# Taking the decision on the range checks ahead of the last products, with an order of pieces from a table

## The chip, the cores and the metric

The kernel runs on one core of a Trainium2 chip. Its engines work side by side and are released by semaphores: TensorE (matmuls), VectorE, ScalarE and GpSimd (elementwise work), SyncE (which issues the transfers). The metric is the time of one execution on the device in microseconds; the median of three runs before the change was 409.76 us (409.35 to 410.42). One further execution was profiled, and its span is 408.4 us.

## The reference

Attention over four batches, eight heads, 768 positions and 64 elements per head, with a causal window of 128 positions and four sink positions that every query sees, and behind it a gated unit that mixes along the positions. All tensors are float32.

```
scores = q @ k.T / sqrt(64)           # kept: sinks (pos < 4), and 0 <= rel < 128
x      = softmax(scores) @ v          # heads side by side: (4, 768, 512)
h      = max(x @ w_in, 0)             # w_in 512 x 1024
u, v   = h[..., :512], h[..., 512:]
v_n    = (v - mean(v)) / sqrt(var(v) + 1e-6)
v_s    = w_spatial @ v_n + b_spatial[:, None]   # along the 768 positions
out    = (u * v_s) @ w_out            # w_out 512 x 512
```

## The kernel before

The kernel has two paths. The fast path assumes four sinks, a window of 128 and values in a range in which a pair of half-precision numbers, a high part and a rest, can stand for a float32: a product is then three half-precision matmuls (high by high, high by rest, rest by high; `three`, line 744). The pairs are made by elementwise operations: the high part is a cast (line 713 on ScalarE, 722 on GpSimd, one of VectorE's own), the rest is a subtraction (line 729, on VectorE or GpSimd). The general path (`general_path`, line 71) does everything in float32 and is taken only if a check fails.

The fast path works through the batches and through tiles of 128 positions: scores against the window and the sinks (`sc`, line 1027 and 1033), a masked maximum in one VectorE pass (`pexp`, `nm`, line 1038), the exponential on ScalarE, the split of the weights (`p`), their transposition, the product with the values (`av`), division (`x`), and the two halves of the hidden layer (`ps_v`, `ps_u`). When a batch is complete, the product along the positions (`ps_s`, on 128x256 tiles), the gate (`g`, lines 1275 and 1279), the product with w_out (`ps_o`, 12 matmuls for one tile of 128 positions), ScalarE's copy of it (`ob`, line 1301) and the store (line 1302) follow. `ps_v`, `ps_u`, `ps_s`, `ps_o` and the small results of the checks share two banks of PSUM in turn; `ob` has three buffers.

The range checks (`checks`, line 874) gather maxima and sums. Their end is a chain: `all_max` (line 772) finds the largest gate bound with a matmul into `ps_row` (line 780), a reduction on VectorE (784), a matmul into `ps_col` (787) and a copy (791); `late` compares (897 to 900); `count` adds the marks of all partitions with a matmul (903); `decide` (908 to 914) turns them into one integer, `flagi`. After the fast path every engine reads `flagi` into a register (line 1370) and `tc.If` (line 1371) branches over the general path.

What sets the order: every operation is a piece in the class `Plan`, with a rank, the engines it can run on, a duration on each by a model, the tiles it reads and writes, and the function that emits it. `forward` (line 391) lists the pieces in the order in which a model of the engines, of the buffers, of a shared port and of TensorE's clock would take them, the lowest priority number first, and picks the engine for pieces that can run on several. `settle` (line 541) calls it with widening tolerance. In `order` (line 520) the priorities are the ranks at first; then a list of 120 seeds, `PASSES`, scatters them and `backward` (line 489) replaces them by distances to the end, 161 times in all. The functions are then called in the resulting order under a manual schedule. 24 pieces of four `idle` matmuls each (line 1310) may be put in where the plan has nothing for TensorE.

Of the kernel before, what the change touches and what calls it, by code (L numbers as in the profile page):

```python
# [270 lines left out]
CHECKS_AT = 56.0  # L271
COLD_TIMES, DMA_START, DMA_LAND = 2.0, 1.7, 1.5
# [4 lines left out]
PASSES = ((360001144, 275, 149, 2), (360001145, 532, 116, 3), (360001147, 406, 76, 2), (360001148, 636, 53, 4), (360001094, 148, 0, 2), (360001096, 596, 486, 4), (360001098, 13, 170, 1), (360001101, 565, 463, 3), (360001223, 680, 71, 3), (360001233, 210, 0, 2), (360001254, 0, 242, 4), (360001255, 0, 145, 5), (360001275, 0, 627, 4), (360001389, 1103, 11, 4), (360001407, 165, 0, 2), (360001474, 33, 0, 5), (360001509, 242, 108, 3), (360001612, 0, 216, 2), (360001663, 0, 118, 1), (360001619, 305, 0, 4), (370001122, 81, 0, 0), (370001124, 68, 0, 0), (370001138, 0, 23, 2), (370001140, 0, 51, 0), (370001149, 60, 0, 0), (370001150, 80, 0, 0), (370001153, 159, 4, 0), (370001154, 207, 37, 0), (370001160, 0, 48, 0), (370001161, 0, 90, 0), (370001162, 0, 115, 0), (370001163, 0, 116, 0), (370001168, 63, 0, 0), (370001171, 157, 0, 0), (370001174, 82, 0, 0), (370001175, 356, 0, 0), (370001178, 121, 79, 0), (370001181, 33, 31, 0), (370001197, 83, 0, 0), (370001198, 22, 0, 0), (370001201, 246, 141, 0), (370001204, 36, 82, 0), (370001206, 138, 136, 0), (370001216, 90, 0, 0), (370001279, 20, 20, 0), (370001296, 256, 89, 0), (370001312, 136, 0, 0), (370001330, 0, 86, 0), (370001374, 3, 4, 0), (370001379, 0, 45, 0), (370001419, 90, 24, 0), (370001423, 115, 98, 0), (370001426, 0, 44, 0), (370001955, 0, 54, 0), (370001960, 284, 0, 0), (370001962, 316, 0, 0), (370001964, 38, 0, 0), (370002082, 101, 0, 0), (370002095, 127, 277, 0), (370002206, 59, 0, 0), (372001153, 0, 24, 0), (372001159, 0, 90, 0), (372001181, 0, 69, 0), (372001191, 184, 0, 0), (372001263, 14, 0, 0), (372001285, 171, 0, 0), (372001297, 0, 90, 0), (372001303, 0, 14, 0), (372001313, 103, 36, 0), (372001322, 0, 74, 0), (372001324, 0, 46, 0), (372001326, 0, 129, 0), (372001327, 0, 125, 0), (372001334, 55, 0, 0), (372001436, 114, 25, 0), (372001441, 0, 28, 0), (372001451, 311, 0, 0), (372001463, 91, 136, 0), (372001543, 0, 9, 0), (372001544, 44, 0, 0), (372001561, 0, 67, 0), (372001566, 0, 184, 0), (372001572, 131, 0, 0), (372001576, 33, 198, 0), (372001583, 138, 45, 0), (372001663, 0, 13, 0), (372001696, 382, 212, 0), (372001701, 337, 19, 0), (372001708, 0, 24, 0), (372001727, 281, 120, 0), (372001797, 277, 74, 0), (372001807, 0, 109, 0), (372001808, 120, 0, 0), (372001817, 193, 94, 0), (372001820, 105, 86, 0), (372001824, 0, 88, 0), (372001826, 0, 104, 0), (372001837, 274, 0, 0), (372001847, 78, 81, 0), (372001929, 72, 0, 0), (379001144, 260, 0, 0), (379001145, 180, 0, 0), (379001239, 0, 33, 0), (379001867, 105, 0, 0), (379001876, 197, 27, 0), (379001902, 192, 11, 0), (379001904, 0, 38, 0), (379002017, 87, 57, 0), (379002028, 0, 173, 0), (379002029, 0, 30, 0), (379002031, 0, 53, 0), (379002044, 214, 29, 0), (379002126, 0, 19, 0), (379002155, 47, 0, 0), (379002158, 250, 0, 0), (379002163, 191, 80, 0), (379002302, 51, 0, 0), (379002303, 177, 0, 0), (379002414, 0, 109, 0), (379002429, 48, 187, 0),)  # L277
NAMES = ("PE", "d", "a", "p", "SP")
# [30 lines left out]


def scatter(seed, i):

    if seed >> 5 & 1 and mix(seed + 555, i) < 0.4:
        return 0.0
    return mix(seed, i)


def near(seed, x):

    if seed >> 6 & 1:  # L320
        return 1.0
    u = (mix(seed, 7) + 1) / 2
    return 1.0 if abs(x - u * u * 430.0) < 5.0 + 20.0 * (mix(seed, 8) + 1) else 0.0


def mix(seed, i):
    x = (seed * 2654435761 + i * 40503 + 12345) & 0xFFFFFFFF
    x ^= x >> 16
    x = x * 2246822519 & 0xFFFFFFFF
    x ^= x >> 13  # L330
    x = x * 3266489917 & 0xFFFFFFFF
    x ^= x >> 16
    return (x & 0xFFFF) / 65536.0 + (x >> 16) / 65536.0 - 1.0


class Plan:
# [54 lines left out]
    def forward(self, prio, ahead, most):  # L391
        ps, n = self.ps, len(self.ps)
        missing, ready = list(self.missing), [0.0] * n
        left = {b: len(u) for b, u in self.users.items()}
        until, taken, since, after = dict.fromkeys(self.users, 0.0), set(), {}, {}
# [6 lines left out]
        follow = [list(x) for x in self.after]  # L402
# [18 lines left out]
        while open_:  # L421
# [38 lines left out]
            for base, ring in self.tiles[i]:  # L460
                if base in taken:
                    if base in after:
                        for j in self.users[after[base]]:
                            follow[j].append(i)
                else:
# [4 lines left out]
                    if slots[ring][k]:  # L470
                        after[base] = slots[ring][k]
                        for j in self.users[slots[ring][k]]:
                            follow[j].append(i)
                    slots[ring][k] = base
# [11 lines left out]
        self.last = start, length, lag, engine, order, follow  # L486
        return max(until.values())

    def backward(self):
        start, length, lag, engine, order, follow = self.last  # L490
        n = len(order)
        earlier, missing = [[] for _ in range(n)], [0] * n
        for i, x in enumerate(follow):
            x = set(x)
            x.discard(i)
            missing[i] = len(x)
            for j in sorted(x):
                earlier[j].append(i)
        ready, free, to_end = [0.0] * n, dict.fromkeys(NAMES, 0.0), [0.0] * n
        open_ = [i for i in range(n) if not missing[i]]  # L500
        for i in open_:
            ready[i] = lag[i]
        while open_:
            best = None
            for i in open_:
                t = max(ready[i], free[engine[i]])
                if best is None or t < best[0] - 1e-9 or (t < best[0] + 1e-9 and start[i] + length[i] > start[best[1]] + length[best[1]]):
                    best = (t, i)
            t, i = best
            to_end[i] = free[engine[i]] = t + length[i]  # L510
            open_.remove(i)
            for j in earlier[i]:
                ready[j] = max(ready[j], to_end[i] + lag[j])
                missing[j] -= 1
                if not missing[j]:
                    open_.append(j)
        last = max(to_end)
        return [last - x for x in to_end]

    def order(self):  # L520

        self.prepare()
        kinds, kind = {}, {}
        for p in self.pieces:
            name, which = ((p[6] or p[5])[0])[:2]
            key = name, str(which[0] if isinstance(which, tuple) else which), p[2] if isinstance(p[2], str) else ""
            kind[p[1]] = kinds.setdefault(key, len(kinds))
        self.end = self.settle([p[0] for p in self.ps])
        prio = [p[0] for p in self.ps]
        for seed, of_kind, of_piece, passes in PASSES:  # L530
            for k in range(max(passes, 1)):
                if passes:
                    prio = self.backward()
                if k == 0:
                    prio = [x + near(seed, x) * (of_kind / 100.0 * scatter(seed, kind[p[1]]) + of_piece / 100.0 * scatter(seed + 7936, 100000 + p[1]))
                            for x, p in zip(prio, self.ps)]
                self.end = self.settle(prio)
        start, length, lag, engine, order, follow = self.last
        return [(self.ps[i][4], engine[i]) for i in order]
# [67 lines left out]
def fast_path(tc, st, scalars, qk, v, v0, vs, w_in, w_sp, w_rows, b_sp, b_col, w_out, out):  # L607
# [7 lines left out]
    with (  # L615
# [738 lines left out]
        checks()  # L1354
        for k in range(FILLERS):
            keep_clock(k)
        order = plan.order()
        with tc.manual_schedule():
            for f, e in order:
                f(e)  # L1360


def tile_kernel(tc, qk, v, v0, vs, n_sink, window, w_in, w_sp, w_rows, b_sp, b_col, w_out, out):
    nc = tc.nc
# [55 lines left out]
```

## Time and profile before

| | |
|---|---|
| runs (3) | 409.35, 409.76, 410.42 us |
| profiled execution, its span | 408.4 us; its own time is not listed |
| median of the runs less that span | 1.36 us |
| TensorE busy | 393.5 us, 96% of the span |
| VectorE, ScalarE, GpSimd busy | 322.4, 298.5, 158.4 us |
| instructions | 10037 |

The page shows TensorE busy in nearly every slice. A group of instructions has a count, its busy time, the mean duration of one, and the idle time of the engine just before it with what ended it. Matmuls overlap, so that the mean of one times the count is more than the busy time. A queue name such as SPq or PEldq is the engine's sequencer, which handles loads of registers, branches and semaphores; these don't count as busy. The timeline gives starts from the begin of the span.

### The profile page before, as it was taken

What the parts mean: (1) busy time and instruction counts of PE and PEld (TensorE: products, weight loads), DVE (VectorE), ACT (ScalarE), POOL (GpSimd) and SP (SyncE); (2) the same over time, 40 slices, a digit from 0 to 9 for tenths busy, and PEclk for the clock granted to TensorE, in tenths of its full rate; (3) what the DMA queues carried; (4) which work ended last, traced back from release to release, by engine and by line L of the source; (5) the groups of instructions that cost most, each with busy time, mean ns of one, the idle gap of its engine ahead of it and who ended that gap; (6) DMA issues with size and microseconds to landing.
All of it is one profiled execution on the core that took longest, in us unless ns stands there. A gap on an engine that the chain in (4) does not pass through costs nothing.

```text
span 408.4 us, 10037 instructions
## 1 busy us (share of the span) xinstructions
PE 393.5 (96%) x3739; PEld 282.2 (69%) x3739; DVE 322.4 (79%) x903; ACT 298.5 (73%) x699; POOL 158.4 (39%) x202
## 2 busy tenths in 40 slices
PE   8999999999999999999999999999999999999991
PEld 6787657767865575758668586777677667687750
DVE  2999999999999989789889894798995892345511
ACT  3998889998988998978999996877644843452220
POOL 4366445563562353557318522255322441100000
PEclk9999899999999999999999999999999999999997
DMA  8999579968586999996989539565444673510211
GB/s 250 335 318 298 173 193 165 178 120 236 129 162 160 240 223 195 187 190 131 207 211 159 95 90 228 121 141 129 86 108 108 137 133 76 185 39 2 91 58 53
DMA packets 128088, 64.73 MB, mean 158 GB/s; under 512 B 109472, under 2 KB 113312, under 8 KB 128032
## 3 DMA queue, kind: packets, MB, share of 16 engines
q1 hardware_dynamic: 128032, 64.02, 67.9%
q8 instruction: 31, 0.51, 0.5%
q14 instruction: 25, 0.20, 0.1%
HBM read 31.10 MB, written 6.29 MB: 92 GB/s over the span
## 4 chain that ended last, share of the span: by engine, by line
PE 67%; DVE 25%; issue 3%; ACT 2%; DMA 1%; DVEq 0%; ACTq 0%
PE ps_s L747 19%; PE ps_o L747 13%; PE ps_u L747 11%; PE ps_v L747 10%; DVE pexp L1038 5%; PE sc L1033 4%; DVE p L729 3%; PE av L1141 2%; PE idle L1310 2%; PE av L1142 2%; PE av L1143 2%; DVE x L1165 1%; DMA qkraw<-qk_t 1%; DVE w L816 1%; DVE vr L1229 1%
## 5 line engine op out<-in xcount | busy, mean ns | idle before, releaser
L747 PE MATMUL ps_s<-wsp,vn 128*128 128x256 f16 x864 | 99.4, 273 | 1.0 <-ACT ob L1301 1.0
L1043 ACT ACTIVATE pexp<-pexp,nm 128x260 f32<-128x260 f32 (+1 forms) x192 | 82.0, 483 | 22.3 <-DVE nm L1038 21.8
L747 PEld LDWEIGHTS <-vn 128*128 128x128 f16 x864 | 83.1, 98 | 15.1 <-issue 4.2
L747 PE MATMUL ps_u<-xT,win 128*128 128x256 f16 x576 | 68.0, 273 | 0.7 <-ACT vr L1205 0.7
L747 PE MATMUL ps_v<-win,xT 128*128 128x512 f16 x288 | 66.3, 381 | 0.0
L747 PE MATMUL ps_o<-wout,g 128*128 128x512 f16 x288 | 65.6, 380 | 0.1
L747 PEld LDWEIGHTS <-win 128*128 128x128 f16 x576 | 55.0, 98 | 10.8 <-issue 2.5
L729 DVE TENSOR_TENSOR p<-pexp,p 128x1024 f16<-128x1024 f32 (+2 forms) x61 | 51.5, 861 | 0.4 <-ACT p L713 0.4
L747 PEld LDWEIGHTS <-xT 128*128 128x128 f16 x288 | 27.6, 98 | 30.4 <-issue 1.2
L747 PEld LDWEIGHTS <-g 128*128 128x128 f16 x288 | 27.4, 98 | 30.6 <-issue 0.7
L729 POOL TENSOR_TENSOR x<-x,x 128x512 f16<-128x512 f32 x24 | 31.1, 1296 | 33.4 <-ACT x L713 32.7
L713 ACT CAST p<-pexp 128x32 f16<-128x32 f32 (+2 forms) x61 | 36.3, 621 | 0.7
L713 ACT CAST g<-g 128x256 f16<-128x256 f32 x37 | 14.9, 402 | 28.0 <-DVE g L1279 25.8
L1221 POOL TENSOR_TENSOR rs<-rs,mhalf 128x1 f32<-128x1 f32 x24 | 19.9, 830 | 36.6 <-DVE rs L1215 31.0
L1275 DVE SCALAR_TENSOR_TENSOR g<-ps_s,b_bc 128x256 f32<-128x256 f32 x48 | 20.2, 421 | 15.4 <-PE ps_s L747 15.1
L1141 PE MATMUL av<-vring,pT 128*128 128x65 f16 x296 | 31.0, 193 | 0.9 <-DVE x L1165 0.9
L1143 PE MATMUL av<-vring,pT 128*128 128x65 f16 x296 | 30.9, 193 | 0.0
L1142 PE MATMUL av<-vring,pT 128*128 128x65 f16 x296 | 30.9, 193 | 0.0
L1141 PEld LDWEIGHTS <-pT 128*128 128x128 f16 x296 | 27.3, 97 | 3.0 <-issue 1.8
L1033 PE MATMUL sc<-kring,qp 64*128 64x260 f16 (+1 forms) x432 | 28.2, 263 | 0.0
L1254 ACT ACTIVATE u<-ps_u 128x256 f32<-128x256 f32 x48 | 18.2, 379 | 13.4 <-PE ps_u L747 13.3
L1142 PEld LDWEIGHTS <-pT 128*128 128x128 f16 x296 | 27.1, 97 | 0.7
(154 smaller groups left out, 737.3 us busy)
## 6 DMA issues: line engine op xcount, KB each, us to landing
qkraw<-qk_t SPq DMA_DIRECT2D x18, 512.0 KB, 4.1
out<-ob SPq DMA_DIRECT2D x24, 256.0 KB, 2.4
vraw<-v_s SPq DMA_DIRECT2D x20, 256.0 KB, 4.1
dec<-w_in SPq DMA_DIRECT2D x8, 512.0 KB, 7.2
wrow<-w_sp_rows SPq DMA_DIRECT2D x6, 384.0 KB, 3.9
dec<-w_out SPq DMA_DIRECT2D x4, 512.0 KB, 4.6
qkraw<-qk_t SPq DMA_DIRECT2D x6, 256.0 KB, 4.8
wsp<-qk_t SPq DMA_DIRECT2D x6, 256.0 KB, 5.1
```

The lines of the kernel that those rows point to most:

```text
L713: nc.scalar.copy(o, x)
L729: eng[e].tensor_tensor(out=o, in0=x, in1=hi, op=ALU.subtract)
L747: nc.tensor.matmul(o, a, m, start=(i == 0), stop=(i == n - 1))
L1033: nc.tensor.matmul(o, qp[rows, qi, hp, :], keys(kring[:, ki], rows), start=(m == 0), stop=(m == 2))
L1038: nc.vector.tensor_tensor_reduce(out=po, in0=o, in1=mask, scale=-0.125 if whole(b) else -0.125 / Q_SCALE ** 2, scalar=3.0e38, op0=ALU.add, ...
L1043: nc.scalar.activation(po, po, AF.Exp, bias=nm()[:, h2 + q:h2 + q + 1], scale=-1.0)
L1141: nc.tensor.matmul(o[:, h], ph, vh, start=(t < 2 and j == 0), stop=False)
L1142: nc.tensor.matmul(o[:, h], ph, vl, start=False, stop=False)
L1143: nc.tensor.matmul(o[:, h], pl, vh, start=False, stop=(j == nb - 1 and (t < 2 or h == HH - 1)))
L1221: nc.gpsimd.tensor_tensor(out=vals["rs", i], in0=vals["rs", i], in1=mhalf, op=ALU.pow)
L1254: plan.add(r + WHEN["u relu"], "a", 0.37, lambda e: nc.scalar.activation(tl("u", (b, c0))[:, d, :], tl("ps_u", i)[:, :TC], AF.Relu, scale= ...
L1275: nc.vector.scalar_tensor_tensor(out=g(), in0=tl("ps_s", i)[:, :TC], scalar=1.0 / (SP_SCALE * VNS), in1=b_bc[:, t0:t0 + TC], op0=ALU.mult, ...
```

## The change

The list of seeds, `backward` and the helpers that scattered are removed. A table `TURNS` of 1868 numbers, one for each piece, gives the priorities of one `settle`; `order` now returns the model's end of each piece and what it writes as well. In the loop that emits the pieces the flag is read, and a hint on the branch is given on all engines, ahead of the first piece whose end in the model is 3.0 us or more behind that of the decision. The branch itself stays at the end. Its label links it to the hint, and it prefers one block for falling through.

```diff
+KNOWN_AFTER = 3.0
...
-PASSES = ((360001144, 275, 149, 2), (360001145, 532, 116, 3), ...
+TURNS = tuple(int(x) for x in """
+-930 63 689 -1263 1416 1530 961 432 520 1957 857 1674 1689 1861 1770 3489 2231 2318 929 1833 ...
...
     def order(self):
...
-        self.end = self.settle([p[0] for p in self.ps])
-        prio = [p[0] for p in self.ps]
-        for seed, of_kind, of_piece, passes in PASSES:
-            for k in range(max(passes, 1)):
-                if passes:
-                    prio = self.backward()
...
-                self.end = self.settle(prio)
-        start, length, lag, engine, order, follow = self.last
-        return [(self.ps[i][4], engine[i]) for i in order]
+        self.end = self.settle([x / 100.0 for x in TURNS] if TURNS else [p[0] for p in self.ps])
+        start, length, lag, engine, order = self.last
+        return [(self.ps[i][4], engine[i], start[i] + length[i], self.ps[i][6]) for i in order]
...
         order = plan.order()
+        known = next(end for _, _, end, writes in order if ("decision", 0) in writes) + KNOWN_AFTER
+        flag = None
         with tc.manual_schedule():
-            for f, e in order:
+            for f, e, end, _ in order:
+                if flag is None and end >= known:
+                    flag = nc.values_load(scalars.flagi[0:1, 0:1], min_val=0, max_val=1)
+                    tc.mark_branch_hint_location("general", flag, engines=list(nc.engines))
                 f(e)
+        return flag
...
-        rv = nc.values_load(scalars.flagi[0:1, 0:1], min_val=0, max_val=1)
-        with tc.If(rv > 0):
+        with tc.If(flag > 0, preferred_fallthrough_block=True, label="general"):
             general_path(tc, scalars.wf, qk, v, w_in, w_sp, b_sp, w_out, out)
```

In the order of the instructions the end of the program shows it. On TensorE the program ended, before, with the last product, the three small matmuls of the checks, the flag read and the branch:

```order
L747 LDWEIGHTS g_6432
L747 MATMUL ps_o<-wout,g_6432 128x512
L780 LDWEIGHTS allmax_m
L780 MATMUL ps_row<-ident_106,allmax_m 1x128
L787 LDWEIGHTS ones
L787 MATMUL ps_col<-allmax_6471,ones 128x1
L903 LDWEIGHTS ones
L903 MATMUL ps_row<-marks,ones 1x26
L1370 TENSOR_LOAD flagi
L1371 COMPARE_AND_BRANCH
```

All checks stood behind the last `ps_o`. Now, on the same engine, the first two of them stand between two tiles of `ps_o`:

```order
L741 LDWEIGHTS g_6198
L741 MATMUL ps_o<-wout,g_6198 128x512
L774 LDWEIGHTS allmax_m
L774 MATMUL ps_row<-ident_106,allmax_m 1x128
L781 LDWEIGHTS ones
L781 MATMUL ps_col<-allmax_6380,ones 128x1
L741 LDWEIGHTS g_6276
L741 MATMUL ps_o<-wout,g_6276 128x512
```

The product behind them starts a new tile and needs the bank that ScalarE's copy of an earlier tile sets free. Twelve `ps_o` later comes the count, and then products along the positions:

```order
L741 LDWEIGHTS g_6225
L741 MATMUL ps_o<-wout,g_6225 128x512
L897 LDWEIGHTS ones
L897 MATMUL ps_row<-marks,ones 1x26
L741 LDWEIGHTS vn
L741 MATMUL ps_s<-wsp,vn 128x256
```

There are 18 of these `ps_s` matmuls between the count and the flag read, where nothing stood before. The read and the hint follow on the same engine:

```order
L741 LDWEIGHTS vn
L741 MATMUL ps_s<-wsp,vn 128x256
L1357 TENSOR_LOAD flagi
L1415 BRANCH_PREFETCH_HINT
L741 LDWEIGHTS g_6276
L741 MATMUL ps_o<-wout,g_6276 128x512
```

Behind the hint there are 36 `ps_o` matmuls, the last three tiles of the output, and then the branch, with nothing between the last product and it. On VectorE the decision was the last work; now one gate piece (a `ps_s` tile times `u`, and its split) stands behind the read and the hint. On SyncE, before, five stores came ahead of the read:

```order
L1302 DMA out<-ob 128x512
L741 DMA wrow<-w_sp_rows 128x768 x5
L1302 DMA out<-ob 128x512
L741 DMA wrow<-w_sp_rows 128x768
L1302 DMA out<-ob 128x512 x5
L1370 TENSOR_LOAD flagi
L1371 COMPARE_AND_BRANCH
```

SyncE could read the flag only when it had issued the last store. Now the read and two register operations stand between the stores:

```order
L1296 DMA out<-ob 128x512
L735 DMA wrow<-w_sp_rows 128x768 x6
L1296 DMA out<-ob 128x512 x3
L1357 TENSOR_LOAD flagi
L1415 BRANCH_PREFETCH_HINT
L1357 ISA x2
L1296 DMA out<-ob 128x512 x3
L1370 COMPARE_AND_BRANCH
```

Three stores of output tiles are queued behind the read. Line numbers of the changed kernel are lower by six in most of the fast path (741 for 747, 1296 for 1302). Over the whole program VectorE has two subtractions `p` of 128x1024, two of `vn` and four of `g` fewer, and GpSimd has as many more; ScalarE has three casts of `vn` and two of `g` fewer. Ahead of the first scores TensorE has 24 `idle` matmuls, where it had 32. All 96 are ahead of the first scores of the second batch in both.

## Rows read from the trace of the kernel before

**Rows 1.** The page: span, busy tenths in 40 slices, groups (count, busy, mean)
```profile
span 408.4 us, 10037 instructions
...
PE   8999999999999999999999999999999999999991
...
L747 PE MATMUL ps_s<-wsp,vn 128*128 128x256 f16 x864 | 99.4, 273 | 1.0 <-ACT ob L1301 1.0
...
L747 PE MATMUL ps_o<-wout,g 128*128 128x512 f16 x288 | 65.6, 380 | 0.1
```

**Rows 2.** TensorE by stretch: window, length, busy, clock, DMA share, GB/s
```profile
7.50:67.70 60.20, 58.09 (x463) 0.97 0.92 261
67.70:399.06 331.36, 328.63 (x3246) 1.00 0.66 143
```

**Rows 3.** TensorE's waits: waiting line, releaser, us in total, times, longest
```profile
PE tr L1072 <- DVE nm L1038: 2.0, 3, 0.8
...
PE ps_s L747 <- ACT ob L1301: 1.0, 1, 1.0
```

**Rows 4.** TensorE's timeline at the start: start, us, line, tile, count
```profile
1.18 6.38 PE L1310 MATMUL idle<-any 128*128 128x256 bf16 x32 [1.18 <-DVE first L563]
...
8.13 1.05 PE L1310 MATMUL idle<-any 128*128 128x256 bf16 x8
```

**Rows 5.** TensorE's timeline from 398.9 to 400 us
```profile
398.68 0.38 PE L747 MATMUL ps_o<-wout,g 128*128 128x512 f16 x1
398.99 0.22 PE L780 MATMUL ps_row<-ident,allmax_m 128*1 128x128 bf16 x1
399.58 0.16 PE L787 MATMUL ps_col<-allmax,ones 1*128 1x1 bf16 x1 [0.37 <-DVE allmax L784]
```

**Rows 6.** Timeline of all engines from 396 to 409 us
```profile
399.14 0.60 ACT L1301 ACTIVATE ob<-ps_o 128x512 f32<-128x512 f32 x1 [1.99 <-PE ps_o L747]
...
400.64 0.17 PE L903 MATMUL ps_row<-marks,ones 128*1 128x26 bf16 x1 [0.91 <-DVE marks L900]
...
401.62 0.14 DVE L914 CAST flagi<-found_any 1x1 int32<-1x1 f32 x1
```

**Rows 7.** Line 1370, flag read: ns min/median/max, first to last start
```profile
L1370 PEldq TENSOR_LOAD <-flagi x1: 492/492/492, 401.8 to 401.8; - x1
```

**Rows 8.** Line 1371, the branch, same columns
```profile
L1371 SPq EVENT_SEMAPHORE  x8: 17/17/17, 402.8 to 403.4; - x8
...
L1371 PEldq COMPARE_BRANCH  x1: 4358/4358/4358, 402.4 to 402.4; - x1
```

**Rows 9.** Line 1416, the end of the program, same columns
```profile
L1416 SPq EVENT_SEMAPHORE  x10: 17/28/1999, 403.8 to 407.8; - x10
...
L1416 SPq DRAIN  x3: 7/7/13, 407.0 to 407.3; - x3
```

**Rows 10.** DMA queues from 402 to 408.4 us: packets, MB, share
```profile
q8 instruction: 2, 0.03, 3.0%
```

**Rows 11.** The tile ob, 380 to 409 us: stores and landing
```profile
L1302 SPq DMA_DIRECT2D out<-ob x5: 332/333/343, 383.5 to 399.8; - x5
...
DMA to landing us min/median/max: 2.0/2.0/4.2
```

**Rows 12.** VectorE's groups by form: count, busy us, mean ns, idle before
```profile
L729 DVE TENSOR_TENSOR p<-pexp,p 128x1024 f16<-128x1024 f32 x29 | 37.9, 1309 | 0.4 <-ACT p L713 0.4
...
L729 DVE TENSOR_TENSOR vn<-vr,vn 128x512 f16<-128x512 f32 x20 | 15.8, 800 | 1.5 <-ACT vn L713 1.4
...
L729 DVE TENSOR_TENSOR g<-g,g 128x256 f16<-128x256 f32 x27 | 12.3, 456 | 6.9 <-ACT g L713 5.5 <-POOL g L722 1.4
```

**Rows 13.** GpSimd's groups by form, same columns
```profile
L729 POOL TENSOR_TENSOR g<-g,g 128x256 f16<-128x256 f32 x21 | 20.7, 986 | 10.7 <-ACT g L713 10.0
...
L729 POOL TENSOR_TENSOR p<-pexp,p 128x1024 f16<-128x1024 f32 x5 | 10.7, 2132 | 5.3 <-ACT p L713 5.0
...
L729 POOL TENSOR_TENSOR vn<-vr,vn 128x512 f16<-128x512 f32 x4 | 4.7, 1172 | 0.2
```

More of the change, by code (lines that the diff above doesn't have):

```diff
@@ L278 @@
+TURNS = tuple(int(x) for x in """
[72 rows of a table added]
+""".split())
 NAMES = ("PE", "d", "a", "p", "SP")
@@ L308 @@
     pass
[L311 to L333, printed above, removed]
 class Plan:
@@ L394, in forward @@
         left = {b: len(u) for b, u in self.users.items()}
-        until, taken, since, after = dict.fromkeys(self.users, 0.0), set(), {}, {}
+        until, taken, since = dict.fromkeys(self.users, 0.0), set(), {}
         slots = {r: [None] * k for r, k in self.rings.items()}
@@ L401, in forward @@
         start, length, lag, engine, order = [0.0] * n, [0.0] * n, [0.0] * n, [""] * n, []
-        follow = [list(x) for x in self.after]
         def room(i):
@@ L460, in forward @@
             for base, ring in self.tiles[i]:
[L461 to L465, printed above, removed]
+                if base not in taken:
                     taken.add(base)
@@ L469, in forward @@
                     since[base] = until[slots[ring][k]] if slots[ring][k] else 0.0
[L470 to L473, printed above, removed]
                     slots[ring][k] = base
@@ L485, in forward @@
             raise RuntimeError("plan: pieces left")
-        self.last = start, length, lag, engine, order, follow
+        self.last = start, length, lag, engine, order
         return max(until.values())
-    def backward(self):
-        start, length, lag, engine, order, follow = self.last
[L491 to L518, printed above, removed]
@@ L520, in order @@
     def order(self):
         self.prepare()
[L523 to L527, printed above, removed]
-        self.end = self.settle([p[0] for p in self.ps])
-        prio = [p[0] for p in self.ps]
-        for seed, of_kind, of_piece, passes in PASSES:
-            for k in range(max(passes, 1)):
-                if passes:
-                    prio = self.backward()
-                if k == 0:
-                    prio = [x + near(seed, x) * (of_kind / 100.0 * scatter(seed, kind[p[1]]) + of_piece / 100.0 * scatter(seed + 7936, 100000 + p[1]))
-                            for x, p in zip(prio, self.ps)]
-                self.end = self.settle(prio)
@@ L538, in order @@
-        start, length, lag, engine, order, follow = self.last
-        return [(self.ps[i][4], engine[i]) for i in order]
+        self.end = self.settle([x / 100.0 for x in TURNS] if TURNS else [p[0] for p in self.ps])
+        start, length, lag, engine, order = self.last
+        return [(self.ps[i][4], engine[i], start[i] + length[i], self.ps[i][6]) for i in order]
     def settle(self, prio):
@@ L1368, in tile_kernel @@
             scalars = Scalars(nc, top, n_sink, window)
-            fast_path(tc, st, scalars, qk, v, v0, vs, w_in, w_sp, w_rows, b_sp, b_col, w_out, out)
-        rv = nc.values_load(scalars.flagi[0:1, 0:1], min_val=0, max_val=1)
-        with tc.If(rv > 0):
+            flag = fast_path(tc, st, scalars, qk, v, v0, vs, w_in, w_sp, w_rows, b_sp, b_col, w_out, out)
+        with tc.If(flag > 0, preferred_fallthrough_block=True, label="general"):
             general_path(tc, scalars.wf, qk, v, w_in, w_sp, b_sp, w_out, out)
```

1 line of the change is left out of this document (removed), and 72 rows, old and new, of the table TURNS.

## The prediction

> **What bounds the kernel now.** I read the page first, then the busy time of TensorE by stretch, then its waits, then the two ends of the timeline. The page's slices show TensorE busy nine tenths or more in every slice but the first and the last [rows 1]: it sets the pace, and the last slice, ten microseconds long, is nearly empty. The table by stretch sharpens this. From the first scores at 7.50 us to the last product's end at 399.06 us TensorE is idle for 60.20 − 58.09 = 2.11 us in the first stretch and 331.36 − 328.63 = 2.73 us in the second, 4.84 us together [rows 2]. No order of the same matmuls can win more than that between these two points, but for what the clock changes. The waits name 2.0 us of it: transposes that wait for VectorE's score pass, in three places of up to 0.8 us [rows 3]. Before 7.50 us TensorE runs 32 idle matmuls, 6.38 us in all [rows 4].
>
> Then the end. The last product ends at 399.06 us, since its start is 398.68 and it takes 0.38 [rows 5]; the span ends at 408.40 [rows 1]. So 9.34 us lie behind the last product, and this is what the reader is to see in the two timelines of the end. First the checks run in a chain between TensorE and VectorE: the row matmul at 398.99, the column matmul at 399.58 [rows 5], the count of marks at 400.64, the decision's last instruction from 401.62 to 401.76 [rows 6]. Then every engine reads the flag, 0.49 us on TensorE's queue from 401.8 [rows 7], and branches over the general path. TensorE's branch takes 4.36 us from 402.4, to 406.8 [rows 8], and after it 408.4 − 406.8 = 1.6 us are left for the closing semaphores and drains, SyncE's among them [rows 9], up to the span's end. Two packets of instructions move on one instruction queue, 0.03 MB, during this [rows 10]. Meanwhile the last tile of the output was long gone: ScalarE copied it from 399.14 to 399.74 [rows 6] and its store was issued at 399.8 with a median landing of 2.0 us [rows 11], so about 401.8. The store was no part of the end.
>
> **Part A, the tail.** The change puts the decision, the flag read and a branch hint ahead of the last 36 products; only the compare and branch stay behind them. So from behind the last product go the chain of checks (399.06 to 401.76, 2.70 us), the flag read and what surrounds it (401.76 to 402.4, 0.6 us), and, if the hint does what its name says, TensorE's 4.36 us branch. What is late next is the store, which was covered. Counted from the end of the last product: the copy is done and the store issued at +0.74 (399.8 − 399.06), landed at +2.74 by the median of five [rows 11]. SyncE then clears eight semaphores, which took 0.6 us (402.8 to 403.4) [rows 8]; half of them can be done before the store lands, so +3.04. Its closing line has ten more [rows 9], of which I take eight at the same 0.08 us, +3.7. From SyncE's first drain at 407.0 to the end at 408.4 [rows 9] it is 1.4 us, so the end is at +5.1. Saved: 9.34 − 5.1 = 4.2 us. Bounds: the slowest store in the row landed after 4.2 us [rows 11], which makes the tail 7.3 and the saving 2.0; if all semaphores but the last few are done while the store flies, the tail is 4.3 and the saving 5.0. I take 4.2, with the median store.
>
> **Part B, what now stands in the stream.** The same instructions are executed earlier, and where TensorE is the bound each stall counts. The row and column matmuls stand in the middle of the products: the column matmul waits 0.37 us for VectorE's reduction [rows 5], and both take banks of the ring that the products use, so the next product waits for ScalarE's copy of a tile, 0.60 us [rows 6] and some 0.1 to start, 0.7. I take the larger alone, since the copy runs beside the reduction: 0.7; the one wait for such a copy that the trace has is 1.0 [rows 3], the upper bound. The count of marks is one matmul of 0.17 us [rows 6]. Its chain on VectorE, from 400.64 to 401.76 or 1.12 us, stood in the open; now 18 spatial products stand between the count and the flag read. At 99.4 / 864 = 0.115 us each [rows 1] they cover 2.1 us, so the flag is there when TensorE's queue gets to it. If that cover were gone TensorE would wait 1.1 us. The flag read stops TensorE's queue for 0.49 us [rows 7]; behind it the remaining products are queued, and so nothing fills it. The hint has no row in the trace: its lower bound is nothing, its upper another flag read, 0.49, and the nearest row of an instruction that only the sequencer handles is a semaphore's 17 ns [rows 8]; I take 0.05. Sum: 0.7 + 0.17 + 0.49 + 0.05 = 1.4 us, between 0.2 (the copies come early, the read hides behind queued matmuls) and 2.2 (1.0 for the copy, the hint at the cost of a read). On the other queues: behind the flag read on ScalarE stand the copies of the last tiles, on SyncE three stores, and on VectorE the last gating operations; each is held up by half a microsecond with 36 products, 36 × 65.6 / 288 = 8.2 us [rows 1], in front of the end, so it costs nothing more.
>
> In sentences apart: the Trainium skill, "Runtime: NRT & Kernel Launch", section "Instruction fetch mechanics", puts a register load at about 200 ns. The row here shows 0.49 us, so it doesn't agree. By the page's figure the sum would be 0.3 us lower, 404.7; the row decides.
>
> **Part C, the order.** A table replaces the seeded passes, so nearly all of the stream moves by some places. The multiset of TensorE's instructions is the same; both orders place all 96 idle matmuls ahead of the second batch. What changes is who does the splitting: VectorE loses two of the 1309 ns subtractions, two of 800 ns and four of 456 ns [rows 12], and these go to GpSimd, where they take 2132, 1172 and 986 ns [rows 13]. VectorE gets lighter by 2.6 + 1.6 + 1.8 = 6.0 us, less small additions, and it was VectorE that TensorE's largest wait, 2.0 us, named [rows 3]. In front only 24 idle matmuls precede the first scores instead of 32; each of those takes 6.38 / 32 = 0.20 us there and 1.05 / 8 = 0.13 later [rows 4], so at most 0.5 us comes back by moving eight. Bounds: −4.84 us if the new order leaves no idle time [rows 2]; above, if every moved operation stands in the path of TensorE and is slower by the difference of its rows, 2 × 0.82 + 2 × 0.37 + 4 × 0.53 = +4.5 us. The nearest row is the wait on VectorE's score pass; I take that for gone and nothing else, −2.0.
>
> **The sum.** Against the profiled execution: 408.40 − 4.2 + 1.4 − 2.0 = 403.6 us of span. The median of the three runs, 409.76, lies 1.36 us above that span; I take the same on top, 405.0 us.
>
> **Rivals.**
> First, the hint gives nothing. For it speaks that what the hint fetches may be overwritten by the instructions of the 36 products behind it, and that the trace has only a branch without hint; against it that the branch takes 4.36 us and the products behind the hint 8.2, so there is time to fetch. Then the branch follows the last product within 0.1 us, takes 4.36 us (402.4 to 406.8 with its ends), and 1.6 us follow: a tail of 6.0 instead of 5.1, 405.9 us. The checks and the read are gone from the tail all the same, so even this is faster.
> In sentences apart: the same section of the Trainium skill says that prefetch is purely sequential and that a taken branch to a page outside the window forces a fetch before execution goes on. The 4.36 us and the two packets of instructions [rows 8, 10] agree with it for a branch without a hint; no run yet shows one with a hint.
> Second, the order gives nothing: the gaps at the score pass are replaced by others as large. For it speaks that TensorE was already busy for 98.8% between the two points, against it VectorE's lighter load. C is 0: 407.0 us.
> Third, the order removes nearly all idle time. C is −4.84: 408.40 − 4.2 + 1.4 − 4.84 + 1.36 = 402.1 us. Against it: some waits sit at the start, where data come in.
> Fourth, slower: the split operations moved to GpSimd starve TensorE. GpSimd takes 1.5 to 2.2 times as long for the same tile [rows 12, 13], and where its result is the next operand TensorE waits the difference. The price is +4.5 instead of −2.0: 411.4 us. It decides if TensorE's idle time between the first scores and the last product grows from 4.84 by over 4.1 us, beyond 8.9. Against it: VectorE, which the longest wait names [rows 3], is relieved by as many operations.
>
> **How the numbers follow.** Chances: the forecast 0.46, no use of the hint 0.14, no gain by order 0.22, all idle time gone 0.11, starved 0.07. A measurement of this kernel can tell about 0.3%, 1.2 us, from no change: faster is below 408.5, slower above 411.0. The forecast and the first and third rival are faster at every bound but the worst of A and B together; of the second about a tenth falls within, with B at 2.2 and A at 2.0; of the fourth two thirds are slower. That makes 0.90 faster, 0.05 same, 0.05 slower. The range goes from 401.8, a little beyond the third rival, to 408.3, which just holds the second rival with A at 3.0 (408.2) and the forecast with A at 2.0 and B at 2.2 (408.0); it leaves out the fourth and half of the third.
>
> **What would show it.** Right: the end of the last product to the end of the span near 5 us, with a short branch on TensorE and SyncE's closing semaphores waiting for the last store; one wait of about 0.7 us for ScalarE's copy behind the column matmul; TensorE's queue stopped for half a microsecond at the flag read; the wait of transposes for the score pass smaller than 2.0 us. Wrong: a branch of 4 us at the end (first rival), idle time of TensorE between the first scores and the last product still near 4.84 without the stalls of B (second), or above 8.9 (fourth), or a wait for the decision at the flag read that is longer than the products ahead of it cover.

## The result and the profile after

The changed kernel takes 404.58 us in the median of four runs (404.07 to 405.48), against 409.76: a ratio of 0.9874 (0.9853 to 0.9895), or 5.2 us less. 405.0 was forecast. Its profiled execution was the run of 404.07 us, with a span of 402.2. Outside the span lie 1.9 us now; in the runs of before they were 1.4 to 1.6, so that the spans alone show some 0.4 us too much gain.

The page, span and slices, as in [rows 1], with VectorE's slices beside TensorE's:

```profile
span 402.2 us, 10061 instructions
...
PE   8999999999998999989999999999999999999995
...
DVE  3999999999999999979889867788988683244430
```

The last slice of TensorE is half full, where it was nearly empty. TensorE's timeline of the end answers to [rows 5, 6]:

```profile
383.64 0.22 PE L774 MATMUL ps_row<-ident,allmax_m 128*1 128x128 bf16 x1
384.23 0.16 PE L781 MATMUL ps_col<-allmax,ones 1*128 1x1 bf16 x1 [0.37 <-DVE allmax L778]
384.40 2.75 PE L741 MATMUL ps_o<-wout,g 128*128 128x512 f16 x12
387.08 0.17 PE L897 MATMUL ps_row<-marks,ones 128*1 128x26 bf16 x1
387.58 2.14 PE L741 MATMUL ps_s<-wsp,vn 128*128 128x256 f16 x18 [0.33 <-DVE found L903]
389.56 7.93 PE L741 MATMUL ps_o<-wout,g 128*128 128x512 f16 x36
```

Here the reader is to see three things. The row and column matmuls take 384.40 − 383.64 = 0.76 us out of the products, 0.37 of them a wait for VectorE's reduction (`allmax`). The count takes 387.58 − 387.08 = 0.50 us, 0.33 of them a wait for VectorE's reading of the count's bank (`found`). And from 387.58 to the last product's end at 397.49 there is no gap, although the flag read and the hint stand in the middle. This is the read on TensorE's queue, which answers to [rows 7], in nanoseconds and with the start at the end of the line:

```profile
L1357 PEldq TENSOR_LOAD <-flagi x1: 682/682/682, 388.2 to 388.2; - x1
```

It is longer than before, 0.68 us from 388.2, but 18 products had been handed to the engine ahead of it and ran on to 389.72. The branch (line 1370, for [rows 8]) and the closing line (1415, for [rows 9], with the hint):

```profile
L1370 SPq EVENT_SEMAPHORE  x8: 17/17/17, 399.1 to 400.8; - x8
...
L1370 PEldq COMPARE_BRANCH  x1: 397/397/397, 393.5 to 393.5; - x1
...
L1370 PEldq EVENT_SEMAPHORE  x1: 51/51/51, 397.5 to 397.5; - x1
...
L1370 SPq COMPARE_BRANCH  x1: 73/73/73, 398.6 to 398.6; - x1
```

```profile
L1415 SPq EVENT_SEMAPHORE  x10: 17/28/28, 400.9 to 402.1; - x10
...
L1415 PEldq BRANCH_PREFETCH_HINT  x1: 44/44/44, 389.0 to 389.0; - x1
```

TensorE's branch takes 0.40 us, not 4.36, and it is taken at 393.5, four microseconds ahead of the last product's end: the sequencer, which handles branches, is that far ahead of the engine. TensorE's next semaphore, at 397.5, waits for the products. The stores of the output, for [rows 11]:

```profile
L1296 SPq DMA_DIRECT2D out<-ob x6: 332/332/344, 377.9 to 398.2; - x6
...
DMA to landing us min/median/max: 2.0/2.0/2.1
```

The last store is issued at 398.2 and lands 2.1 us later, at 400.3; SyncE's eight semaphores end 0.5 us behind that, at 400.8, and the closing line at 402.1. The tail is 402.2 − 397.49 = 4.7 us, and the store sets it. Last, TensorE's waits, for [rows 3]:

```profile
PE sc L1027 <- DVE nm L1032: 1.3, 2, 1.2
PE ps_u L741 <- ACT vr L1199: 1.3, 1, 1.3
...
PE av L1148 <- DMA vring<-v_ones: 0.5, 1, 0.5
PE tr L1081 <- DVE nm L1032: 0.4, 1, 0.4
PE ps_col L781 <- DVE allmax L778: 0.4, 1, 0.4
...
PE ps_s L741 <- DVE found L903: 0.3, 1, 0.3
```

The transposes' wait for the score pass is 0.4 us where it was 2.0, but scores now wait 1.3 us for the same pass, and other waits have gone and come.

### The profile page after: what moved, and what is told of

Read it like the earlier page. It is cut to its first block, busy times and chain, and to the rows that moved or that the text cites. A ratio compares the mean times of both kernels' runs of the same rounds, so it can differ in the third digit from the quotient of the medians.

```text
span 402.2 us, 10061 instructions
## 1 busy us (share of the span) xinstructions
PE 391.3 (97%) x3739; PEld 280.4 (70%) x3739; DVE 316.0 (79%) x896; ACT 296.6 (74%) x696; POOL 164.1 (41%) x212
## 5 line engine op out<-in xcount | busy, mean ns | idle before, releaser
L1037 ACT ACTIVATE pexp<-pexp,nm 128x260 f32<-128x260 f32 (+1 forms) x192 | 83.1, 483 | 13.4 <-DVE nm L1032 12.4
L723 DVE TENSOR_TENSOR p<-pexp,p 128x16 f16<-128x16 f32 (+2 forms) x60 | 46.2, 781 | 7.1 <-ACT p L707 5.9
L723 POOL TENSOR_TENSOR g<-g,g 128x256 f16<-128x256 f32 x25 | 20.8, 832 | 39.1 <-ACT g L707 38.6
L707 ACT CAST g<-g 128x256 f16<-128x256 f32 x35 | 14.0, 401 | 30.4 <-DVE g L1273 30.3
L1215 POOL TENSOR_TENSOR rs<-rs,mhalf 128x1 f32<-128x1 f32 x24 | 18.3, 763 | 44.2 <-DVE rs L1209 41.0
```

Of the source, the lines that this page charges most:

```text
L707: nc.scalar.copy(o, x)
L723: eng[e].tensor_tensor(out=o, in0=x, in1=hi, op=ALU.subtract)
L1037: nc.scalar.activation(po, po, AF.Exp, bias=nm()[:, h2 + q:h2 + q + 1], scale=-1.0)
L1215: nc.gpsimd.tensor_tensor(out=vals["rs", i], in0=vals["rs", i], in1=mhalf, op=ALU.pow)
```

## The experiments

Ratios are to the kernel before, run on the same chip, with 95% intervals.

**Checks last.** The new order, with the old tail.

```diff
-        known = next(end for _, _, end, writes in order if ("decision", 0) in writes) + KNOWN_AFTER
+        late = (("ps_row", "gate"), ("1", "gate"), ("ps_col", "gate"), ("r", "gate"), ("marks", 0), ("ps_row", "marks"), ("decision", 0))
+        order = [p for p in order if p[3][:1] != () and p[3][0] not in late or p[3] == ()] + [p for p in order if p[3] and p[3][0] in late]
...
+        rv = nc.values_load(scalars.flagi[0:1, 0:1], min_val=0, max_val=1)
+        with tc.If(rv > 0):
```

> The new order from the table, but the chain of checks stands behind the last product again and the flag is read at the end, without a hint. Theory (the order alone brings the last product forward, from 399.06 to about 396.6 us without the checks in the stream, and the old tail of 9.3 us follows): span 405.9, time about 407.3 us, ratio 0.994. Rival (the order is worth nothing, all the gain is in the tail): 409.8 us, ratio 1.000.

Measured: 407.24 us, 0.9938 (0.9916 to 0.9961). TensorE's first scores, its end and its branch:

```profile
6.40 0.71 PE L1021 MATMUL sc<-wsp,qkraw 64*128 64x128 f32 x8
...
389.10 7.93 PE L741 MATMUL ps_o<-wout,g 128*128 128x512 f16 x36
...
398.62 0.17 PE L897 MATMUL ps_row<-marks,ones 128*1 128x26 bf16 x1 [0.91 <-DVE marks L894]
```

```profile
L1368 PEldq COMPARE_BRANCH  x1: 4138/4138/4138, 400.4 to 400.4; - x1
```

The last product ends at 397.03, two microseconds earlier than before, and the old tail follows, with its long branch. The order alone is worth 2.5 us (1.6 to 3.4); the rival is out.

**Early checks in the old order.** The order from the seeds; the chain stands ahead of the last three tiles and the read and hint ahead of the last one. In the cut, `head_` holds the row matmul, the reduction, the column matmul, the copy and the marks, and `None` stands for the flag read and the hint.

```diff
+        head_ = [("ps_row", "gate"), ("1", "gate"), ("ps_col", "gate"), ("r", "gate"), ("marks", 0)]
...
+            if key == ("ps_s", (3, 2, 3)):
+                new += [by_key[k] for k in head_]
+            new.append(p)
+            if key == ("ps_s", (3, 2, 3)):
+                new.append(by_key["ps_row", "marks"])
+            if key == ("g2", (3, 2, 3), 1):
+                new.append(by_key["decision", 0])
+            if key == ("ps_o", (3, 2, 0)):
+                new.append(None)
```

> The order of before, but the chain of checks is moved in front of the last three tiles of the output and the flag read with its hint in front of the last one. Theory (the tail shrinks from 9.3 to 4.7 us, the checks cost the stream 0.9 us): 406.0 us, ratio 0.991. Rival (the gain is in the order alone): 409.8 us, ratio 1.000.

Measured: 406.68 us, 0.9928 (0.9903 to 0.9954), about 3 us less. The timeline of TensorE, from the row matmul on:

```profile
389.14 0.22 PE L780 MATMUL ps_row<-ident,allmax_m 128*1 128x128 bf16 x1
...
391.95 0.17 PE L903 MATMUL ps_row<-marks,ones 128*1 128x26 bf16 x1
392.54 7.93 PE L747 MATMUL ps_o<-wout,g 128*128 128x512 f16 x36 [0.41 <-DVE g L1275]
```

The stream pays 0.76 us for the first two matmuls and 0.17 for the count, and 0.41 for a gate that came late behind the decision. The tail is 405.1 − 400.47 = 4.6 us. With the run before, 2.5 + 3.0 = 5.5 us: the two halves add up to the 5.2 that the whole change gave, within their intervals. TensorE's branch in this kernel:

```profile
L1394 PEldq COMPARE_BRANCH  x1: 2636/2636/2636, 396.4 to 396.4; - x1
```

Here the branch has its hint, and yet takes 2.64 us. The hint was given at 395.3, 1.1 us ahead of the branch; in the changed kernel it was 4.5 us ahead (389.0 and 393.5), and the branch took 0.40. It ends at 399.0, ahead of the last product's end at 400.47, and adds nothing to the tail.

**No hint.** The changed kernel without the line of the hint and with a plain `tc.If(flag > 0)`.

```diff
-                    tc.mark_branch_hint_location("general", flag, engines=list(nc.engines))
...
-        with tc.If(flag > 0, preferred_fallthrough_block=True, label="general"):
+        with tc.If(flag > 0):
```

> The changed kernel with the early flag read, but without the hint and the label. Theory (TensorE's branch begins 4 us ahead of the last product's end, so its 4.4 us end before the last store lands, hint or not): 404.6 us, ratio 0.987, the branch itself back at about 4.4 us. Rival (the hint saves the branch time at the end): 405.5 to 406.3 us, ratio 0.990 to 0.992.

Measured: 405.42 us, 0.9897 (0.9863 to 0.9930). Line 1369, the branch, on TensorE's queue:

```profile
L1369 PEldq COMPARE_BRANCH  x1: 3775/3775/3775, 394.7 to 394.7; - x1
...
L1369 PEldq EVENT_SEMAPHORE  x1: 51/51/51, 398.8 to 398.8; - x1
```

Without the hint the branch is long again, 3.78 us, but it begins at 394.7 and ends at 398.5, beside products that end at 398.76. The tail is 403.7 − 398.76 = 4.9 us, 0.2 more than with the hint. The stores:

```profile
DMA to landing us min/median/max: 2.0/2.2/2.3
```

The last store is the one of 2.3 us, against 2.1 in the changed kernel, and this is the 0.2: from its landing it is 0.5 us to the end of SyncE's eight semaphores and 1.4 more to the end of the span in both. The medians differ by 0.8 us, but the intervals overlap widely, and the profiles place the larger part ahead of the last product. So the hint does shorten the branch, tenfold, but no gain in time from that is shown here.

**Read late.** The changed kernel with checks early, but read and branch at the end without a hint, as before.

```diff
+        rv = nc.values_load(scalars.flagi[0:1, 0:1], min_val=0, max_val=1)
+        with tc.If(rv > 0):
```

> The changed kernel with the checks early, but the flag read at the end as before, and without a hint. Theory (TensorE's sequencer runs ahead of its products by about 4 us, so that its read and its branch of 4.4 us go beside them, and only the last store sets the end): 404.6 to 405.3 us, ratio 0.987 to 0.989. Rival (the branch follows the last product, 0.5 + 4.4 + 1.6 us instead of 4.7): 406.5 us, ratio 0.992.

Measured: 406.06 us, 0.9906 (0.9874 to 0.9938), runs from 403.43 to 407.99, too wide to tell the theories apart. The profile does. Line 1366 on TensorE's queue:

```profile
L1366 PEldq COMPARE_BRANCH  x1: 3322/3322/3322, 397.4 to 397.4; - x1
...
L1366 PEldq EVENT_SEMAPHORE  x1: 51/51/51, 400.8 to 400.8; - x1
```

The branch runs from 397.4 to 400.7, and the last product ends at 400.62: even here it is beside the products. The tail is 406.2 − 400.62 = 5.6 us, not 6.5 as a branch behind the last product would make it. It is 0.9 us longer than in the changed kernel, and the store is the reason:

```profile
DMA to landing us min/median/max: 2.0/2.0/3.0
```

The last store is the one of 3.0 us. SyncE's read, at 391.4, stood well ahead; ScalarE's, at 400.7, and its branch, at 401.3, were over before the store landed at 404.3, and behind the landing come the same 0.5 and 1.4 us. Why the last store landed later in the two kernels without a hint isn't shown.

**Read at once.** `KNOWN_AFTER = 0.0` in the changed kernel. This puts the read ahead of the decision in the program. The flag then holds only what was known of sinks and window, so that in this kernel the range checks can't choose the general path.

> The changed kernel with KNOWN_AFTER 0: flag read and hint follow the count directly on TensorE's queue, ahead of the 18 spatial products. Theory (a read that is ready costs TensorE nothing because the sequencer runs ahead; here it waits for the decision and nothing is queued ahead of it): a gap of TensorE of about 1.7 us instead of 0.3 behind the count, 406.0 us, ratio 0.991. Rival (the read costs 0.5 us wherever it stands, and the wait for the decision 1.1 us): a gap of 1.1 us, as the read was paid before, 405.4 us, ratio 0.990.

Measured: 405.41 us, 0.9888 (0.9863 to 0.9912). The gap behind the count stayed at 0.33 us, and the read began at 387.2, before the count at 389.01:

```profile
L1357 PEldq TENSOR_LOAD <-flagi x1: 650/650/650, 387.2 to 387.2; - x1
```

It waited for nothing and no gap stands at it; the wait that the expectations were about wasn't made. The next run makes it.

**The read waits.** The decision is emitted right behind the count, and the read and hint right behind the decision.

```diff
+        decision = next(p for p in order if ("decision", 0) in p[3])
+        order = [q for p in order if p is not decision for q in ([p, decision] if ("ps_row", "marks") in p[3] else [p])]
...
+                f(e)
+                if ("decision", 0) in writes:
+                    flag = nc.values_load(scalars.flagi[0:1, 0:1], min_val=0, max_val=1)
```

> The changed kernel with the decision emitted right behind the count, and flag read and hint right behind the decision, ahead of the 18 spatial products, so that TensorE's queue holds nothing that the read could wait beside. Theory (a read stops TensorE's queue until the decision is there, 0.95 us, and 0.7 us more; 18 products cover that in the changed kernel): a gap of 1.7 us behind the count instead of 0.3, 406.0 us, ratio 0.991. Rival (matmuls behind the read start without it): a gap of 0.3 us, 404.6 us, ratio 0.987.

Measured: 406.34 us, 0.9919 (0.9891 to 0.9946).

```profile
388.66 0.17 PE L897 MATMUL ps_row<-marks,ones 128*1 128x26 bf16 x1
390.51 2.13 PE L741 MATMUL ps_s<-wsp,vn 128*128 128x256 f16 x18 [1.68 <-DVE flagi L908]
```

TensorE stands still for 1.68 us, as the theory said. So the 18 products in the changed kernel cover all of it, decision and read, except for the 0.33 us of the bank.

**The gap filled.** The kernel before, with eight idle matmuls moved into the 0.8 us gap at 46.9 us.

```diff
+        move = [where["idle", 9], where["idle", 23]]
+        turn = where["tr", (7, 0)]
+        order = [p for n, p in enumerate(order) if n < turn and n not in move] + [order[n] for n in move] + [p for n, p in enumerate(order) if n >= turn and n not in move]
```

> The kernel before, with two of its groups of four idle matmuls (from 39.6 and 49.6 us) moved into the gap at 46.6 us in which TensorE waited 0.8 us for the score pass, and after which its granted clock was 0.50 for some 3 us. Theory (the gap drops the clock, so that about 3 us of work take twice as long): no half clock there any more, 0.8 to 1.6 us less, ratio 0.996 to 0.998. Rival (the fall of the clock has nothing to do with the gap): half clock in the same place, ratio 1.000.

Measured: 409.68 us, 0.9996 (0.9983 to 1.0010). TensorE by stretch (window, length, busy, granted clock), before and with the gap filled:

```profile
47.00:48.00 1.00, 0.33 (x2) 0.86 0.00 0
48.00:49.00 1.00, 1.00 (x7) 0.50 0.93 180
```

```profile
47.00:48.00 1.00, 0.66 (x6) 1.00 0.02 3
48.00:49.00 1.00, 1.00 (x10) 1.00 1.09 209
```

The clock stayed at its upper level (1.00, 2.4 GHz) where it had fallen to the lower one (0.50, 1.2 GHz), so the gap, 0.78 us before and 0.34 now, did drop it. But no time was won. At about 65 us TensorE was 1.1 us ahead of before, and at 98 us no longer (the start of the same matmul in both traces). Its waits with the gap filled:

```profile
PE tr L1072 <- DVE nm L1038: 1.6, 3, 0.6
PE av L1141 <- DVE x L1165: 1.2, 1, 1.2
...
PE ps_s L747 <- ACT ob L1301: 1.0, 1, 1.0
...
PE ps_u L747 <- ACT vr L1205: 0.9, 1, 0.9
```

Before, beside those of [rows 3]:

```profile
PE av L1141 <- DVE x L1165: 0.9, 1, 0.9
PE ps_u L747 <- ACT vr L1205: 0.7, 1, 0.7
```

The four waits add up to 4.7 us, where they were 4.6. My theory was right about the clock and wrong about the time. TensorE alone doesn't set the pace there; what does, this run doesn't show.

**Fewer idle matmuls.** The changed kernel without the last two groups of four, and without the last nine (36 matmuls, 3.9 us of TensorE's time). The cut is the first kernel's; the second has `fill[-9:]`.

```diff
+        fill = [n for n, p in enumerate(order) if p[3] and p[3][0][0] == "idle"]
+        order = [p for n, p in enumerate(order) if n not in fill[-2:]]
```

> The changed kernel without its last two groups of idle matmuls, eight at 53.3 us, 0.9 us of TensorE's time; the rest of the order is the same. Theory (TensorE is the bound from 38 us on, the eight stand in no gap): 0.9 us less, 403.7 us, ratio 0.985. Rival (they fill a wait, or the clock falls without them): no change or slower, ratio 0.987 to 0.991.

> The changed kernel without its last nine groups of idle matmuls, 36 of them between 21 and 54 us, 3.9 us of TensorE's time. Theory (up to 38 us the transfers are the bound, the idle matmuls stand in gaps there; without them the gaps are idle time and the granted clock falls in places): TensorE idle 3 us more, half clock in places, 404 to 406 us, ratio 0.986 to 0.991. Rival (TensorE is the bound from 20 us on): 3.9 us less, 400.7 us, ratio 0.978.

Measured: 404.21 us, 0.9864 (0.9843 to 0.9886), and 403.52 us, 0.9845 (0.9826 to 0.9864). Neither is clear of the change's own 0.9853 to 0.9895, though the second's median is 1.1 us below it and also below my theory's 404 to 406. The rival's 3.9 us are out. In the profile, the slowest of its runs, the kernel without 36 reaches the end of its last product at 397.48 us, 0.01 from the changed kernel's, whose profile is the fastest of its runs. TensorE from 40 to 50 us (columns as with the gap filled), in the changed kernel and without the 36:

```profile
40.00:50.00 10.00, 10.00 (x64) 1.00 0.68 164
```

```profile
40.00:50.00 10.00, 9.41 (x51) 0.83 0.67 189
```

The clock fell there. From the first scores to the last product TensorE is busy for 385.73 us instead of 387.19, only 1.5 us less, and idle for 1.3 us more. So most of the 3.9 us went into a lower clock and into waits. That TensorE wasn't the bound where they stood can't be told apart from a clock that took the gain back.

**The start.** The changed kernel with 32 idle matmuls ahead of the first scores, and without eight (16 ahead). The last line of the cut is the second kernel's.

```diff
+        scores = next(n for n, p in enumerate(order) if p[3] and p[3][0][0] == "sc")
+        move = [n for n in fill if n > scores][:2]
+        order = order[:scores] + [order[n] for n in move] + [p for n, p in enumerate(order) if n >= scores and n not in move]
...
+        order = [p for n, p in enumerate(order) if n not in fill[4:6]]
```

> The changed kernel with the eight idle matmuls that stand behind the first scores moved in front of them, so that 32 stand there as before the change; nothing else differs. Theory (up to 183 us VectorE, 95 to 99% busy, is as much the bound as TensorE, and its work begins with the first scores; a later start is carried to the end): first scores at about 7.0 us instead of 5.3 to 6.4, 405.8 us, ratio 0.990. Rival (TensorE alone is the bound, and moved idle matmuls cost it nothing): 404.6 us, ratio 0.987.

> The changed kernel without the last eight of the 24 idle matmuls in front of the first scores. Theory (the scores' data is there at 5.05 us, the 24 idle matmuls end at 5.2 to 6.3 us): first scores at 5.1 us in every run, 403.8 us, ratio 0.985. Rival (nothing to gain there, or the clock rises later): 404.6 us or more, ratio 0.987.

Measured: 405.40 us, 0.9898 (0.9868 to 0.9927), and 405.15 us, 0.9903 (0.9865 to 0.9941). With 32 the first scores start at 7.36 us, with 16 at 4.91. The longest wait of the latter:

```profile
PE av L1148 <- DMA vring<-v_ones: 2.6, 2, 1.9
```

The 16 start earliest and wait 2.6 us for a transfer instead, 0.5 in the changed kernel. An earlier start didn't bring what I expected; 32 lies between theory and rival, and the start's share in the gain stays open.

**Both fewer.** The changed kernel without those eight and without the 36 (`fill[4:6] + fill[-9:]`).

> The changed kernel without those eight idle matmuls in front and without the 36 between 21 and 54 us. Theory (the early start counts, the 36 count little, since VectorE is the bound there): 402.8 to 403.8 us, ratio 0.983 to 0.985. Rival (without idle matmuls the granted clock falls and takes it back): 404.6 us or more.

Measured: 405.46 us, 0.9884 (0.9851 to 0.9918), runs from 402.26 to 406.15: no gain to be seen. No version was clearly faster than the change.

## Why the prediction was right

**Part A.** The tail was to shrink from 9.34 to 5.1 us; it is 4.7. The path was the one forecast: copy, store, landing, SyncE's semaphores. The step that was mis-sized is SyncE's closing, by 0.4 us: after its eight semaphores, at 400.8, the program ends in 1.4 us, where 0.66 for further semaphores and 1.4 for the drains were added up. Less the 0.4 us that moved outside the span, 4.2 us of time were won, the forecast figure; that the two 0.4 cancel is luck. What was wrong is the part given to the hint. The first rival put a branch without hint behind the last product, with 6.0 us of tail, and the forecast gave the hint the credit for taking 4.36 us away; the run without the hint has a branch of 3.78 us and a tail of 4.9, in which the store is the last to finish. The branch was late before because the decision was late and nothing was left on TensorE to run beside it. With the decision early, the sequencer reaches the branch up to 4 us ahead of the engine (3.2 us in the run that reads late, 4.0 with the hint). The rule of the Trainium skill that the rival stood beside ("Runtime: NRT & Kernel Launch", section "Instruction fetch mechanics": a taken branch outside the window forces a fetch) agrees with the 3.78 us without a hint. The rule says nothing of hints, nor of when the sequencer gets there, and that decided.

**Part B.** Forecast 1.4 us, measured 0.76 + 0.50 = 1.26, from each small matmul's start to the next product's. Behind the near sum three terms were off, and they nearly cancel. The 0.7 for the row and column matmuls was priced as a wait for ScalarE's copy. That wait isn't there: the copy ends at 384.35 and the product starts at 384.40; the 0.76 are the two matmuls and VectorE's reduction between them. The flag read was priced at 0.49 and cost nothing, because the 18 products cover the read and not only the decision; I had let the cover end where the read begins. The count was priced at 0.17 and cost 0.50: the next product needs the bank that VectorE reads, and this wait of 0.33 us wasn't in the sum. Without the cover TensorE would wait 1.1 us, the forecast said; the run that took it away shows 1.68 with the read in it, near 1.1 + 0.49.

**Part C.** Forecast −2.0 us; the order alone gave −2.5 (1.6 to 3.4), about 0.4 of it in the tail (8.6 against 9.3 us in the spans, less the 0.4 outside). The size was near, but the path was only in part the one forecast, so that the near number is partly luck. The forecast took 2.0 us out of TensorE's idle time between the first scores and the last product, 4.84 us before. The rows of the changed kernel and of the one with checks last (window, length, busy; clock, DMA share, GB/s):

```profile
5.32:397.49 392.17, 387.19 (x3716) 1.00 0.70 162
```

```profile
6.40:397.03 390.63, 386.71 (x3714) 1.00 0.70 162
```

The idle time is 5.0 us, 0.7 of it at the checks (0.37 and 0.33), and 3.9 us with checks last: it fell by 0.9, not by 2.0. The wait named, transposes for the score pass, did fall from 2.0 to 0.4 us, and the waits of a product for ScalarE's copy (1.0) [rows 3] and of `av` for VectorE's division (0.9) went as well, but waits of scores for the score pass (1.3) came in their place. The other part is a term that the forecast put at nothing, with at most 0.5 us for it: the start, with eight idle matmuls fewer ahead. The first scores start at 7.50 us before [rows 2], at 6.40 with checks last and at 5.32 in the changed kernel. Of the 399.06 − 397.03 = 2.0 us by which the last product ends earlier with checks last, 1.1 are there already at the first scores. These are single profiles, and the runs on the start don't show that an earlier start is carried to the end: with 16 ahead the first scores start at 4.91 us and the last product ends at 399.28. The forecast's first sentence, that TensorE sets the pace, can be trusted only behind some 183 us, where it was idle for 0.3 us before. VectorE's busy time from 30 to 183 us (columns: window, length, and busy time with count for TensorE, its weight loads, VectorE, ScalarE, GpSimd; clock, DMA share, GB/s), before and after:

```profile
30.00:183.00 153.00, 149.15 (x1455) 105.69 (x1454) 145.81 (x396) 137.95 (x320) 77.15 (x95) 0.99 0.88 190
```

```profile
30.00:183.00 153.00, 149.74 (x1481) 106.41 (x1481) 145.76 (x400) 138.56 (x334) 89.92 (x103) 1.00 0.87 193
```

VectorE is busy for 95% of this stretch in both, TensorE for 97 and 98%. That two engines bound it together would explain that filling a gap of TensorE moved nothing; it is argued and not shown, and ScalarE, at 90%, and the transfers, at 0.88, are near as well. Lightening VectorE, the reason that I gave, is consistent with the gain, but no run took that alone; which part of the 2.5 us it makes, and which the start, stays open.

**Rivals.** That the order gives nothing is out by the time with checks last. By the sign named for it, idle time still near 4.84 us without the stalls of the checks, it wasn't far off: 5.0 − 0.7 = 4.3 us, where the forecast needed 2.84. That the order takes away all idle time did not happen, nor that it starves TensorE, for which the point of decision was 8.9 us. Two of the signs of being right were not seen: no wait for ScalarE's copy behind the column matmul, and no stop at the flag read.

## What to carry to other kernels

Look up when a sequencer reaches an instruction, not when its engine would: here the flag read, the hint and the branch behind queued matmuls left no gap on TensorE, and what made them cost, 1.68 us in one run and most of the old tail, was a value that was decided late. Take the busy time of all engines by stretch before pricing a gap on one: where two were busy for 95% or more, filling a gap on TensorE gained nothing. Price the start as well as the idle time behind it. A small result that shares a bank ring can cost the wait for its reader (0.33 us here), and not only its own matmul.

## What was not expected of the hardware

The number of idle matmuls at the lower rate at the program's start differs from run to run with the same instructions. A group of 24 took 4.21 us in the changed kernel's profile and 5.30 in those without the hint and with checks last; the single matmul goes from 0.21 to 0.11 us at some point between 3.9 and 7.3 us in the fourteen profiles, while the granted clock reads 1.00 for the first ten microseconds. The flag read on TensorE took 0.49 us at the end of a program and behind the late decision, and 0.65 to 0.69 beside running products in nine kernels; in the kernel with early checks in the old order it ran beside products too and took 0.49, so that running products alone don't make the difference. A hint that came 1.1 us ahead of the branch left 2.64 us of it, one 4.5 us ahead 0.40.
